# Issue order of expert weight loads, and a second set of raw buffers for the second expert

## The chip, the cores and the metric

One Trainium2 chip, one core. The time of a kernel is the device time of one execution in microseconds (us); the figure for a kernel is the median of its runs. One further execution is recorded by the profiler; its span runs from its first instruction to its last.

## What is computed

Three stages follow each other. Windowed causal attention over 2 x 8 heads of 576 tokens gives 1152 rows of 512 numbers. A dense mixture of four experts follows, and then a routed mixture of eight, in which a row goes to one expert at most:

```
x = attention(q, k, v)                         # window 64, as rows of 512
x = sum over e of p[:, e] * (relu(x @ w1[e]) @ w2[e])          # 4 experts, all rows
keep = x @ w_skip > 0                          # the others leave as they are
e = argmax(x @ w_gate); g = softmax(x @ w_gate)[e]
out[keep] = x + g * (relu(x @ m1[e]) @ m2[e])  # 8 experts, each with its own rows
```

An expert has a first matrix (512 x 1024) and a second one (1024 x 512), 2 MB each in float32.

## The kernel before

Every product is taken with operands split into a high and a low part (`h` and `l`) of float32r, so each weight matrix is loaded raw and then split. A matrix comes in four chunks of 512 KB (`w_load`, one transfer from SP's queue each). `w_split` then has ScalarE (ACT) copy the chunk to the high part (line 331) and VectorE (DVE) subtract to get the low part (line 335). A raw buffer is free again once its low part is written. There are four raw buffers, `raw`; when the routed stage opens (`open_moe2`, key `"M"`), four more, `raw2`, are opened on memory that the dense stage and the routing held.

Two sets of split weights are used in turn: the even routed experts read `wb`, the odd ones `wa`. The weights of expert e + 1 are split while expert e computes (`w_pass("r", e + 1, 1)`, then `(…, 2)`).

An expert works on blocks of 128 of its rows (`block`). TensorE (PE) takes the first product in two pieces of 512 columns, `mm` (line 897); ACT evicts each to `hr` (line 921); PE transposes it (line 938); ACT and DVE write the high and low part of `ht` (lines 942 and 945); PE takes the second product; DVE adds the gated result into `xg` (line 979). Block 0 stands in the straight code of an expert. Blocks 1 and 2 stand behind a branch (`tails`, lines 1086 and 1088) and only run if the expert has that many rows; a last block of at most 64 rows has a shorter form. With these inputs experts 0, 3, 5 and 6 have block 0 alone, experts 1 and 2 have one block more, expert 4 two, and the last expert has one short block.

Rows of an expert are gathered by GpSimd (POOL) from a copy of `x` in device memory (line 847), transposed by PE (line 363), and the results are scattered to the output (line 855).

**The order on the engines is planned.** Each operation is added with an engine, a cost, what it reads and writes, and a priority. `Plan.run` simulates the engines with these costs, and the instructions are issued in the order of their planned start. A load costs 1.46 us on SP, and its reader may start 1.1 us after it. A cast costs (1024 + 112) / 1200 = 0.947 us. On ACT and DVE an operation of priority 0 or more is held back when it would end over 0.2 us after an urgent one (priority below 0, such as the eviction to `hr`) that is already known to be ready. Everything up to the end of expert 0's block 0 is one plan; each later expert's straight part is a plan of its own, which starts at 0.

In these later plans the loads of a first matrix for experts 3 to 7 (`early`) are planned on a made-up engine `"X"`, where each takes 0.01 us; those of the second matrix are planned on `"SP"`. All are issued on SP's queue, which is in order: a load whose buffer isn't free yet holds back every load behind it. The four early loads start at 0.00, 0.01, 0.02 and 0.03, the first load of the second matrix at 0.00. So SP's order is: first matrix, chunk 0; second matrix, chunk 0; first matrix, chunks 1 to 3; second matrix, chunks 1 to 3.

Which buffers a load uses is set by `extra`: for experts 2 to 7 a counter gives the first matrix `raw` and the second `raw2`. Experts 0 and 1 use `raw` for all of their eight chunks.

The routing has its tiles in two pools: `rc`, which stays, and `rt`, which is closed when the routed stage opens. By the tiles' sizes (bytes per partition) the dense stage's pool gives back 43,008, and the routed stage takes 18,432 and 20,480 of it, so 4,096 are left there: one `raw2` buffer lies on the dense stage's memory (`x2`), and three on that of `rt`.

Of the kernel before, what the change touches and what calls it, by code (L numbers as in the profile page):

```python
# [7 lines left out]
F32 = mybir.dt.float32  # L8
F32R = mybir.dt.float32r
BF16 = mybir.dt.bfloat16  # L10
# [13 lines left out]
E2 = 8  # L24
# [175 lines left out]
def c_dve(n):  # L200
    return (n + 64) / 960.0
# [3 lines left out]
def fused_kernel(ctx: ExitStack, tc: tile.TileContext, q, k, v, dp, w1, w2, wskip, wgate, m1, m2, out):  # L205
# [19 lines left out]
    ps_o = attn.enter_context(tc.tile_pool(name="ps_o", bufs=1, space=PSUM))  # L225

    ident = const.tile([128, 128], F32, name="ident")
    identb = const.tile([128, 128], BF16, name="identb")
    mask = [const.tile([128, 128], BF16, name=f"mask{i}") for i in range(2)]
    mask0 = [const.tile([128, 128], BF16, name=f"mask0{i}") for i in range(2)]  # L230
    fold2 = const.tile([128, 64], F32, name="fold2")
    prob = const.tile([128, TT, E1], F32, name="prob")
    psum1 = const.tile([128, TT], F32, name="psum1")
# [10 lines left out]
        "2h": ringa.tile([128, FC, DM], F32R, name="wa2h"),  # L244
        "2l": ringa.tile([128, FC, DM], F32R, name="wa2l"),
    }
    qz = [qk_p.tile([128, HP, 2, 2, 64], F32, name=f"qz{i}") for i in range(2)]
    kt = [qk_p.tile([128, HP, 3, 64], F32, name=f"kt{i}") for i in range(2)]

# [60 lines left out]
    def w_load(src, part, c, prio, extra=False, early=False):  # L310
        b = (M["raw"] if extra else raw_r).buf()

        def f():
            if part == 1:
                SP.dma_start(out=b.tile, in_=src[c * 128:(c + 1) * 128, :])  # L315
            else:
                SP.dma_start(out=b.tile.rearrange("p (a n) -> p a n", a=2),
                             in_=src[c * 256:(c + 1) * 256, :].rearrange("(a p) n -> p a n", p=128))

        add("X" if early else "SP", 0.01 if early else 1.46, f, rd=["M"] if extra else [], new=[b], prio=prio)  # L320
        return b

    def w_split(b, ring, key, part, c, prio, pool=False, after=(), hpool=False, hdve=False):
# [246 lines left out]
    def open_routing():  # L570
        attn.close()
        ps_r = route_ps.enter_context(tc.tile_pool(name="ps_r", bufs=1, space=PSUM))
        rc_p = ctx.enter_context(tc.tile_pool(name="rc", bufs=1))
        rings[0]["1h"] = rc_p.tile([128, KC, FF], F32R, name="wb1h")
        rings[0]["1l"] = rc_p.tile([128, KC, FF], F32R, name="wb1l")
        rt_p = routing.enter_context(tc.tile_pool(name="rt", bufs=1))
        R["rtp"] = rt_p
        R["tab"] = ps_r.tile([128, TT, 5, E2], F32, name="tab")
        R["lg"] = ps_r.tile([128, 512], F32, name="lg")
        R["pf"] = ps_r.tile([128, 512], F32, name="pf")  # L580
        for nm, sh, dt in (("tri", [128, 128], BF16), ("ones", [128, 128], BF16), ("iota_s", [128, 128], F32),
                           ("iota_e", [128, E2], F32), ("jlow", [128, TT + 1], F32), ("tok1", [128, 1], F32),
                           ("wr", [128, KC, E2 + 1], F32), ("os0", [128, E2], BF16), ("os1", [128, E2], BF16),
                           ("cnt", [128, E2 + 2], I32), ("idg", [128, TT, E2], U32), ("ids", [128, TT, E2], U32), ("id0", [128, 1], U32), ("x0", [128, DM], F32),
                           ("gates", [128, TT, E2], F32), ("tb", [128, TT, 5, E2], F32),
                           ("a", [128, TT, E2], F32), ("b", [128, TT, E2], F32), ("lvw", [1, E2], F32),
                           ("lvt", [1, 6, E2], F32), ("lvx", [1, 6, E2], F32), ("lvs", [1, 2], F32)):
            R[nm] = (rt_p if nm in ("tri", "ones", "iota_s", "iota_e", "jlow", "tok1", "wr", "id0", "x0") else rc_p).tile(
                sh, dt, name=nm)
        for i in range(2):  # L590
            for nm, sh, dt in (("x2t", [128, KC, 128], F32), ("m8", [128, 8], F32),
                               ("i8", [128, 16], U32), ("sc", [128, 8], F32), ("oh", [128, E2], BF16),
                               ("ex", [128, E2], F32), ("tm", [128, E2], F32), ("gj", [128, TT + 1], F32),
                               ("oj", [128, TT], F32), ("r", [128, 128], BF16), ("g", [128, 4], F32),
                               ("gb", [128, 4], BF16), ("w", [128, 5, E2], BF16),
                               ("wx", [128, TT, 5 * E2], BF16)):
                R[nm, i] = rt_p.tile(sh, dt, name=f"{nm}{i}", tag=f"{nm}{i}", bufs=1)
        R["rpr"].pool = rt_p

    def route_consts():  # L600
# [24 lines left out]
    def route(t):  # L625
# [108 lines left out]
        def spread(c0, c1, pr, after=()):  # L734

            e0, n = c0 * E2, (c1 - c0) * E2
            add("DVE", c_dve(TT * n) + 0.01, lambda: DVE.tensor_tensor(
                out=T("wx")[:, :, e0:e0 + n],
                in0=T("w")[:, c0:c1].rearrange("p c e -> p (c e)").unsqueeze(1).to_broadcast([128, TT, n]),
                in1=T("oj").unsqueeze(2).to_broadcast([128, TT, n]), op=ALU.mult),  # L740
                rd=[K("oj")] + [K("w0")] * (c0 == 0) + [K("w1")] * (c1 == 5), wr=[K(("wx", c0))], prio=pr)
            add("PE", max(0.11, TT * n / 2400), lambda: PE.matmul(
                out=R["tab"].rearrange("p j c e -> p j (c e)")[:, :, e0:e0 + n], lhsT=T("r"), rhs=T("wx")[:, :, e0:e0 + n],
                start=(t == 0), stop=(t in (GT, TT - 1)), skip_group_check=True),
                rd=[K("r"), K(("wx", c0)), *after], wr=[("tab", c) for c in range(c0, c1)], prio=pr, slack=sl)

# [41 lines left out]
    def route_end():  # L788
        o = R_os(TT - 1)

        def idx():
            tb, a = R["tb"], R["a"]
            DVE.tensor_scalar(out=tb[:, :, 1], in0=R["tab"][:, :, 1], scalar1=128.0, scalar2=-1.0, op0=ALU.mult, op1=ALU.add)
            DVE.tensor_tensor(out=a, in0=tb[:, :, 1], in1=R["tab"][:, :, 0], op=ALU.add)
            DVE.tensor_scalar(out=R["idg"], in0=a, scalar1=0.0, scalar2=None, op0=ALU.max)

        add("DVE", 0.45, idx, rd=[("tab", 0), ("tab", 1)], wr=["idg"], prio=-1)
        for f in later:
            f()
        add("PE", 0.03, lambda: PE.matmul(out=R["pf"][:, 0:E2], lhsT=R["ones"], rhs=R[o], start=True, stop=True),  # L800
            rd=[o], wr=["pf"], prio=-4)

        def num():
            n, x, sm = R["pf"][0:1, 0:E2], R["lvx"], R["lvs"]
            DVE.tensor_tensor(out=x, in0=n.unsqueeze(1).to_broadcast([1, 6, E2]), in1=R["lvt"], op=ALU.is_gt)
            DVE.tensor_reduce(out=sm[:, 1:2], in_=x[:, 5], axis=AX.X, op=ALU.max)
            DVE.scalar_tensor_tensor(out=x, in0=x, scalar=1.0, in1=R["lvw"].unsqueeze(1).to_broadcast([1, 6, E2]),
                                     op0=ALU.mult, op1=ALU.mult, accum_out=sm[:, 0:1])
            DVE.tensor_copy(R["cnt"][0:1, E2:E2 + 2], sm)
            DVE.tensor_copy(R["cnt"][0:1, 0:E2], n)  # L810

        def rest():
            tb, a, b = R["tb"], R["a"], R["b"]
            DVE.tensor_copy(tb[:, :, 2:5], R["tab"][:, :, 2:5])
            DVE.tensor_tensor(out=b, in0=tb[:, :, 2], in1=tb[:, :, 3], op=ALU.add)
            DVE.tensor_tensor(out=R["gates"], in0=b, in1=tb[:, :, 4], op=ALU.add)
            DVE.tensor_scalar(out=b, in0=a, scalar1=0.0, scalar2=4097.0, op0=ALU.is_lt, op1=ALU.mult)
            DVE.tensor_tensor(out=R["ids"], in0=a, in1=b, op=ALU.add)

        add("DVE", 0.84, num, rd=["pf"], wr=["cnt"], prio=16)  # L820
        add("DVE", 1.25, rest, rd=["idg"] + [("tab", c) for c in range(2, 5)], wr=["gates", "ids"], prio=20)


# [163 lines left out]
    def w_pass(kd, e, p, prio=None):  # L987
        if prio is None:
            npass[0] += 1
            prio = 500.0 + 10 * npass[0]  # L990
        src = ((w1, w2) if kd == "m" else (m1, m2))[p - 1][e]
        ring, key = (wa, "wa") if kd == "m" else (rings[e], rkey[e % 2])
        for c in range(4):
            extra = False
            if kd == "r" and e > 1:
                extra = nw[0] % 8 > 3
                nw[0] += 1
            st = KN["w2s"] if (kd, e, p) == ("m", 0, 2) else 2.5
            b = w_load(src, p, c, prio + st * c, extra, early=kd == "r" and e > 2 and p == 1)
            w_split(b, ring, key, p, c, prio + st * c, pool=(kd, e, p) == ("m", 0, 2) and KN["w2pool"][c],  # L1000
                    after=["idg"] if kd == "r" and e == 1 else [])

    nw = [0]

    with tc.manual_schedule():
        w_pass("m", 0, 2, KN["w2p"])
# [158 lines left out]
```

## Time and profile before

| what | value |
|---|---|
| median of 3 runs | 675.88 us (675.45 to 675.97) |
| the profiled execution: time | 672.51 us |
| the profiled execution: span | 670.8 us |
| mean granted clock of TensorE, as a share of full | 0.984 |
| busy share of PE, DVE, ACT, POOL | 94%, 48%, 35%, 14% |

The profiled execution lies 3.37 us below the median, and its span 1.7 us below its time. The busy share of PE is an average: it counts as busy in every slice from about 70 us to 480, where the dense stage ends, and has gaps in the routed stage.

### The profile page before, as it was taken

Reading aid. Unit: us, or ns where it says so; the run is one execution under the profiler, and the core shown is the slowest. Engines: PE = TensorE matmul, PEld = TensorE weight load, DVE = VectorE, ACT = ScalarE, POOL = GpSimd, SP = SyncE. Lnnn points to the kernel's source line nnn. Section 1 sums busy time; section 2 is a strip of 40 time slices with the busy share of each in tenths; the row PEclk is TensorE's granted clock in tenths of the full one; section 3 lists DMA queues with packets and bytes.
Section 4 is the critical chain, followed back from the end, with each engine's and each line's share of the span. In section 5 each row is a group of like instructions: output and inputs, shape, how many; then the busy total and the mean of one; then the engine's idle time right before and its main releaser. Section 6 shows DMA issues by size and latency. Waiting matters only on the chain. (4 is left out here: it accounts for less than half of the span.)

```text
span 670.8 us, 9656 instructions
## 1 busy us (share of the span) xinstructions
PE 628.2 (94%) x3652; PEld 552.8 (82%) x3652; DVE 323.8 (48%) x699; ACT 237.0 (35%) x492; POOL 91.5 (14%) x112
## 2 busy tenths in 40 slices
PE   6889999999999999999999999999987899899783
PEld 6788899898989898989898989898965678687573
DVE  5997932137312136212136336265576575654661
ACT  4974741035202033202033202124326465634550
POOL 6541320000000000000000000000043142312510
PEclk9999999999999999999999999999989999899987
DMA  9668000008300005200004210113339957961631
GB/s 219 159 164 241 23 4 1 0 1 270 106 1 1 0 1 176 75 1 1 0 1 165 87 64 33 48 47 104 129 131 308 360 185 227 303 252 39 209 112 29
DMA packets 55851, 71.69 MB, mean 107 GB/s; under 512 B 32953, under 2 KB 32953, under 8 KB 55776
## 3 DMA queue, kind: packets, MB, share of 16 engines
q1 hardware_dynamic: 52912, 62.17, 29.1%
q0 software_dynamic: 2864, 8.54, 4.4%
q8 instruction: 44, 0.72, 0.4%
q14 instruction: 31, 0.25, 0.1%
HBM read 64.00 MB, written 7.47 MB: 107 GB/s over the span
## 5 line engine op out<-in xcount | busy, mean ns | idle before, releaser
L523 PE MATMUL mm<-xth,wa1h 128*128 128x384 f32 (+1 forms) x416 | 137.4, 330 | 0.0
L523 PE MATMUL mm<-xtl,wa1h 128*128 128x384 f32 (+1 forms) x416 | 135.3, 325 | 0.0
L523 PE MATMUL mm<-xth,wa1l 128*128 128x384 f32 (+1 forms) x416 | 135.2, 325 | 0.0
L529 ACT ACTIVATE hh<-mm 128x384 fp32r<-128x384 f32 (+1 forms) x104 | 48.5, 466 | 234.5 <-PE mm L523 225.9
L544 PE MATMUL mm<-wa2h,hh 128*128 128x512 f32 (+1 forms) x296 | 116.9, 395 | 0.0
L544 PE MATMUL mm<-wa2h,hl 128*128 128x512 f32 (+1 forms) x296 | 115.0, 389 | 0.0
L544 PE MATMUL mm<-wa2l,hh 128*128 128x512 f32 (+1 forms) x296 | 114.9, 388 | 0.0
L531 DVE SCALAR_TENSOR_TENSOR hl<-mm,hh 128x384 fp32r<-128x384 f32 (+1 forms) x104 | 54.5, 526 | 121.7 <-ACT hh L529 121.6
L523 PEld LDWEIGHTS mm<-xth,wa1h 128*128 128x128 f32 x416 | 78.3, 188 | 0.7
L523 PEld LDWEIGHTS mm<-xtl,wa1h 128*128 128x128 f32 x416 | 78.2, 188 | 0.5
L523 PEld LDWEIGHTS mm<-xth,wa1l 128*128 128x128 f32 x416 | 78.2, 188 | 0.0
L544 PEld LDWEIGHTS mm<-wa2h,hl 128*128 128x128 f32 x296 | 55.7, 188 | 12.4
L544 PEld LDWEIGHTS mm<-wa2l,hh 128*128 128x128 f32 x296 | 55.8, 189 | 11.1
L544 PEld LDWEIGHTS mm<-wa2h,hh 128*128 128x128 f32 x296 | 55.8, 188 | 11.0
L556 DVE SCALAR_TENSOR_TENSOR x<-mm,prob,x 128x512 f32<-128x512 f32 (+1 forms) x28 | 20.5, 732 | 91.2 <-PE mm L544 91.2
L766 POOL DMA_INDIRECT x<-scr,id x1 | 1.2, 1242 | 360.3 <-DVE id L783 360.3
L331 ACT CAST wa2h<-raw 128x1024 fp32r<-128x1024 f32 x32 | 33.3, 1053 | 28.0 <-PE mm L544 18.6
L335 DVE TENSOR_TENSOR wa1l<-raw,wa1h 128x1024 fp32r<-128x1024 f32 x31 | 36.9, 1220 | 9.6 <-ACT wa1h L331 9.0
L335 DVE TENSOR_TENSOR wa2l<-raw,wa2h 128x1024 fp32r<-128x1024 f32 x30 | 36.2, 1219 | 7.0 <-ACT wa2h L331 6.8
L331 ACT CAST wa1h<-raw 128x1024 fp32r<-128x1024 f32 x30 | 30.3, 1047 | 22.5 <-DMA raw<-in_moe_w_dram 16.0
L855 POOL DMA_INDIRECT out_dram<-xg,ids x11 | 16.1, 1460 | 86.9 <-DVE xg L979 59.5
L444 POOL TENSOR_TENSOR s<-s,mx 128x512 f32<-128x512 f32 x18 | 20.2, 1122 | 50.1 <-DVE mx L441 23.0
(203 smaller groups left out, 917.8 us busy)
## 6 DMA issues: line engine op xcount, KB each, us to landing
raw<-in_moe_w_dram SPq DMA_DIRECT2D x96, 512.0 KB, 5.5
scr<-x SPq DMA_DIRECT2D x9, 256.0 KB, 2.1
out_dram<-x SPq DMA_DIRECT2D x9, 256.0 KB, 2.3
qn<-in_q_dram SPq DMA_DIRECT2D x8, 256.0 KB, 4.0
kn<-in_k_dram SPq DMA_DIRECT2D x8, 256.0 KB, 4.1
vn<-in_v_dram SPq DMA_DIRECT2D x8, 256.0 KB, 4.7
qn<-in_q_dram SPq DMA_DIRECT2D x2, 128.0 KB, 4.4
kn<-in_k_dram SPq DMA_DIRECT2D x2, 128.0 KB, 4.4
```

The source lines that it names most:

```text
L331: (POOL.tensor_copy if hpool else DVE.tensor_copy if hdve else ACT.copy)(out=aps()[0], in_=b.tile)
L335: (POOL if pool else DVE).tensor_tensor(out=l, in0=b.tile, in1=f32(h), op=ALU.subtract)
L444: add("POOL", 1.0, lambda: POOL.tensor_tensor(out=s.tile, in0=s.tile, in1=mx[:, 3].unsqueeze(2).to_broadcast([128, HP, 128]), op=ALU.mult) ...
L523: PE.matmul(out=ps[:, 0:n], lhsT=wa[a][:, kk, f * 128:(f + 1) * 128], rhs=x[:, kk, g0:g0 + n], start=(i == 0), stop=(i == 3 * KC - 1))
L529: add("ACT", c_act(n), lambda: ACT.activation(out=hh[:, f, 0:n], in_=ps[:, 0:n], func=ACTF.Relu), rd=[ps], wr=[("hh", f)], prio=-1)
L531: add("DVE", c_dve(n), lambda: DVE.scalar_tensor_tensor(out=hl[:, f, 0:n], in0=ps[:, 0:n], scalar=0.0, in1=f32(hh[:, f, 0:n]), op0=ALU.max ...
L544: PE.matmul(out=ps[:, 0:c1 - c0], lhsT=x[:, f, o:o + 128], rhs=wa[a][:, f, c0:c1], start=(f == 0 and i == 0), stop=(f == FC - 1 and i == 2))
L556: DVE.scalar_tensor_tensor(out=z, in0=y, scalar=prob[:, t, e:e + 1], in1=z, op0=ALU.mult, op1=ALU.add)
L766: add("POOL", 1.0, lambda: POOL.indirect_dma_start(out=R["x0"], out_offset=None, in_=scr[0:128 * (GT + 1), :], in_offset=bass.IndirectOffs ...
L855: add("POOL", 1.0, lambda: POOL.indirect_dma_start(out=out, out_offset=bass.IndirectOffsetOnAxis(ap=R["ids"][0:n, j, e:e + 1], axis=0), in ...
```

## The change

The early loads take 0.00 us instead of 0.01 in the plan. The counter is gone: the second matrix of every expert but expert 0 goes into `raw2`, so that expert 1 uses all eight raw buffers as the later ones do. So that `raw2` can be written while the routing is being finished, the routing's tiles that are still in use at that point move from `rt` to `rc` (a new `wy` holds the late part of `wx`); to make room, two masks and an identity move to the pool of the attention, and `tb` is cut from five columns to two, with its sums read from PSUM.

```diff
-    identb = const.tile([128, 128], BF16, name="identb")
-    mask = [const.tile([128, 128], BF16, name=f"mask{i}") for i in range(2)]
-    mask0 = [const.tile([128, 128], BF16, name=f"mask0{i}") for i in range(2)]
+    identb = qk_p.tile([128, 128], BF16, name="identb")
+    mask = [qk_p.tile([128, 128], BF16, name=f"mask{i}") for i in range(2)]
+    mask0 = [qk_p.tile([128, 128], BF16, name=f"mask0{i}") for i in range(2)]
...
-        add("X" if early else "SP", 0.01 if early else 1.46, f, rd=["M"] if extra else [], new=[b], prio=prio)
+        add("X" if early else "SP", 0.0 if early else 1.46, f, rd=["M"] if extra else [], new=[b], prio=prio)
...
-                           ("gates", [128, TT, E2], F32), ("tb", [128, TT, 5, E2], F32),
+                           ("gates", [128, TT, E2], F32), ("tb", [128, TT, 2, E2], F32),
...
-                               ("wx", [128, TT, 5 * E2], BF16)):
-                R[nm, i] = rt_p.tile(sh, dt, name=f"{nm}{i}", tag=f"{nm}{i}", bufs=1)
+                               ("wx", [128, TT, 5 * E2], BF16), ("wy", [128, TT, 3 * E2], BF16)):
+                R[nm, i] = (rt_p if nm in ("x2t", "m8", "i8", "tm", "gj", "wx") else rc_p).tile(sh, dt, name=f"{nm}{i}", tag=f"{nm}{i}", bufs=1)
...
+            wx = lambda: T("wy" if c0 else "wx")[:, :, 0:n]
...
-            tb, a, b = R["tb"], R["a"], R["b"]
-            DVE.tensor_copy(tb[:, :, 2:5], R["tab"][:, :, 2:5])
-            DVE.tensor_tensor(out=b, in0=tb[:, :, 2], in1=tb[:, :, 3], op=ALU.add)
-            DVE.tensor_tensor(out=R["gates"], in0=b, in1=tb[:, :, 4], op=ALU.add)
+            a, b = R["a"], R["b"]
+            DVE.tensor_copy(b, R["tab"][:, :, 2])
+            DVE.tensor_tensor(out=b, in0=b, in1=R["tab"][:, :, 3], op=ALU.add)
+            DVE.tensor_tensor(out=R["gates"], in0=b, in1=R["tab"][:, :, 4], op=ALU.add)
...
-            extra = False
-            if kd == "r" and e > 1:
-                extra = nw[0] % 8 > 3
-                nw[0] += 1
+            extra = kd == "r" and e > 0 and p == 2
```

## Rows read from the trace of the kernel before

**Rows 1.** The page's head: the span.

```profile
span 670.8 us, 9656 instructions
```

**Rows 2.** Waits of PE from 535 us on: total us, times, longest us.

```profile
PE pt L938 <- ACT hr L921: 8.1, 2, 5.4
```

**Rows 3.** Timeline of PE from 560 us: start, us, line, operation, count, idle before.

```profile
560.73 0.51 PE L897 MATMUL mm<-wa1h,xs 128*128 128x512 f32 x1 [0.50 <-PEq L1088]
...
574.20 0.48 PE L897 MATMUL mm<-wb1h,xs 128*128 128x512 f32 x1 [0.23 <-PEq L1086]
...
581.78 1.12 PE L938 MATMUL pt<-ident,hr 128*128 128x128 f32 x4 [2.71 <-ACT hr L921]
...
591.49 0.39 PE L897 MATMUL mmx<-wb1h,xs 128*128 128x512 f32 x1
...
603.52 0.60 PE L363 MATMUL pt<-ident,xj 128*128 128x128 f32 x4
...
615.24 0.39 PE L897 MATMUL mm<-wa1h,xs 128*128 128x512 f32 x1
...
628.53 0.48 PE L897 MATMUL mm<-wb1h,xs 128*128 128x512 f32 x1
...
638.83 1.11 PE L938 MATMUL pt<-ident,hr 128*128 128x128 f32 x4 [5.42 <-ACT hr L921]
...
650.03 0.47 PE L897 MATMUL mm<-wa1h,xs 128*128 128x512 f32 x1 [0.89 <-DVE xg L979]
```

**Rows 4.** Timeline of ACT in expert 6, 628 to 648 us.

```profile
634.54 1.04 ACT L331 CAST wa1h<-raw 128x1024 fp32r<-128x1024 f32 x1 [4.98 <-DMA raw<-in_moe_w_dram]
...
638.19 0.59 ACT L921 ACTIVATE hr<-mm 128x512 f32<-128x512 f32 x1
...
647.08 1.07 ACT L331 CAST wa2h<-raw 128x1024 fp32r<-128x1024 f32 x1
```

**Rows 5.** Timeline of SP's queue, 618 to 632 us: issues, not transfers.

```profile
618.13 0.34 SPq L315 DMA_DIRECT2D raw<-in_moe_w_dram  x1
626.08 0.37 SPq L317 DMA_DIRECT2D raw<-in_moe_w_dram  x1
626.50 1.62 SPq L315 DMA_DIRECT2D raw<-in_moe_w_dram  x3
628.31 3.52 SPq L317 DMA_DIRECT2D raw<-in_moe_w_dram  x3
```

**Rows 6.** Timeline of DVE, 616 to 626 us: the splits of expert 6.

```profile
616.89 4.62 DVE L335 TENSOR_TENSOR wb1l<-raw,wb1h 128x1024 fp32r<-128x1024 f32 x4
...
624.73 1.28 DVE L335 TENSOR_TENSOR wb2l<-raw,wb2h 128x1024 fp32r<-128x1024 f32 x1
```

**Rows 7.** Loads of second matrices issued from 490 to 520 us.

```profile
DMA to landing us min/median/max: 4.6/7.2/12.5
```

**Rows 8.** Timeline of PE from the end of the routing to expert 2.

```profile
485.81 0.61 PE L710 MATMUL mm<-rp,x 128*128 128x128 f32 x4
...
490.86 0.24 PE L742 MATMUL tab<-wx,r 128*128 128x144 bf16 x1
...
507.55 0.47 PE L897 MATMUL mm<-wa1h,xs 128*128 128x512 f32 x1 [2.96 <-PEq L1086]
...
522.29 0.40 PE L897 MATMUL mmx<-wa1h,xs 128*128 128x512 f32 x1
...
536.75 0.51 PE L897 MATMUL mm<-wb1h,xs 128*128 128x512 f32 x1 [0.44 <-PEq L1088]
```

**Rows 9.** Timeline of ACT: a cast in 455:490, an eviction in 490:530.

```profile
467.79 1.05 ACT L331 CAST wa1h<-raw 128x1024 fp32r<-128x1024 f32 x1 [2.91 <-DMA raw<-in_moe_w_dram]
...
490.13 0.60 ACT L921 ACTIVATE hr<-mm 128x512 f32<-128x512 f32 x1 [3.01 <-PE mm L897]
```

**Rows 10.** Timeline of SP's queue: the load of that cast.

```profile
463.32 2.60 SPq L315 DMA_DIRECT2D raw<-in_moe_w_dram  x3
```

**Rows 11.** Branches of line 1086 from 495 to 512 us: count, ns, start.

```profile
L1086 PEldq COMPARE_BRANCH  x1: 6509/6509/6509, 500.9 to 500.9; - x1
```

More of the change, by code (lines that the diff above doesn't have):

```diff
@@ L736, in spread @@
             e0, n = c0 * E2, (c1 - c0) * E2
+            wx = lambda: T("wy" if c0 else "wx")[:, :, 0:n]
             add("DVE", c_dve(TT * n) + 0.01, lambda: DVE.tensor_tensor(
-                out=T("wx")[:, :, e0:e0 + n],
+                out=wx(),
                 in0=T("w")[:, c0:c1].rearrange("p c e -> p (c e)").unsqueeze(1).to_broadcast([128, TT, n]),
@@ L742, in spread @@
             add("PE", max(0.11, TT * n / 2400), lambda: PE.matmul(
-                out=R["tab"].rearrange("p j c e -> p j (c e)")[:, :, e0:e0 + n], lhsT=T("r"), rhs=T("wx")[:, :, e0:e0 + n],
+                out=R["tab"].rearrange("p j c e -> p j (c e)")[:, :, e0:e0 + n], lhsT=T("r"), rhs=wx(),
                 start=(t == 0), stop=(t in (GT, TT - 1)), skip_group_check=True),
@@ L1001, in w_pass @@
                     after=["idg"] if kd == "r" and e == 1 else [])
-    nw = [0]
     with tc.manual_schedule():
```

## Prediction, on record before the changed kernel was seen

> **What bounds the kernel now.** I read the page's head first: a span of 670.8 us in which TensorE counts as busy almost throughout, so only what keeps PE waiting can shorten it [rows 1]. The change touches the routed stage alone, so I took the waits of PE from 535 us on: 8.1 us in two waits of the transposes of line 938 for the eviction `hr` on ACT, the longer of them 5.4 us [rows 2]. The timeline of PE shows where: 2.71 us ahead of 581.78, in expert 4, and 5.42 us ahead of 638.83, in expert 6 [rows 3]. These are the experts that follow one with block 0 alone.
>
> Next, why `hr` is late. In expert 6 ACT evicts `hr` at 638.19, just behind a cast of the next expert's first matrix, and an earlier of those casts had ACT idle for 4.98 us until its load landed [rows 4]. SP's queue says why the load was late: the first chunk of expert 7's first matrix is issued at 618.13, then one of its second matrix at 626.08, and only then, from 626.50, the other three chunks of the first [rows 5]. They had had buffers long before: the low parts that free `raw` are written from 616.89 to 621.51, while the `raw2` buffer on which the queue stood still is freed by the split at 624.73, which lasts 1.28 us [rows 6]. So three loads stood for 5 to 7 us behind a load that they don't need. In expert 4 the order of the queue is the same.
>
> **The early loads at 0.00 us.** The five loads now tie at 0, priority decides, and the first matrix has the smaller numbers: its four chunks come first. No instruction is added or removed; three SP issues move ahead of one, and the one moved back waits for its own buffer until about 626 in any case. POOL's queue isn't touched.
>
> What it is worth is read from whole experts, since a matmul after a wait is slower at first too (four transposes take 1.11 us behind the 5.42 us wait, and 0.60 us at 603.52 [rows 3]). Start to start, experts 3 and 5 take 574.20 - 560.73 = 13.47 and 628.53 - 615.24 = 13.29 us, mean 13.38. Expert 4's block 0 takes 591.49 - 574.20 = 17.29, an excess of 3.91. Expert 6 takes 650.03 - 628.53 = 21.50, of which 0.89 is another wait, for DVE, that stays: an excess of 7.23 [rows 3]. Together **-11.1 us**. From below: if only the waits themselves went, 8.1 [rows 2]. Will the chunks be there? With expert 6's splits ending by 621.5 they would be issued by then, and even the median landing of crowded loads, 7.2 us [rows 7], brings the last at 628.7, when expert 6 begins and ACT takes chunk 0 first.
>
> **`raw2` for expert 1: the gain.** Its second matrix no longer waits for `raw`, and the loads of expert 2's first matrix, which come behind it on SP, find `raw` free earlier. Expert 1's block 0 takes 522.29 - 507.55 = 14.74, 1.36 over the mean; its second block takes 536.75 - 522.29 less the 0.44 of the branch, 14.02 [rows 8], against 603.52 - 591.49 = 12.03 for the same block of expert 4 [rows 3], 1.99 over. With the casts' data there early I take both away: **-3.3 us**. Bounds: none of it, or all.
>
> **`raw2` for expert 1: the price.** This is the part that speaks against the change. The planner believes that the loads land 2.56 us after `"M"` (1.46 + 1.1), so it may put the first cast of `wa2h` at 2.56 to 3.51 us. Block 0's eviction `hr` is planned about 3.38 us after `"M"` (0.264 + 0.2 for the rows' cast, 12 matmuls of 512 columns at 0.215, 0.11 for a table matmul, 0.22 latency). The overrun is 0.13 us, under the 0.2 that the rule allows: the cast goes ahead of `hr` on ACT, and the later casts between the evictions to `ht` and `hr`. All these figures only set the order. What it costs is how late the cast's load lands, for behind it on ACT stand `hr` and `ht` of expert 0, and for those PE's transposes and second product wait.
>
> The load can't go before its buffer is free. The trace doesn't show that wait. From below, the last reader of `x2` ends at 485.81 + 0.61 = 486.4; from above, the last table matmul that reads a tile left in `rt` ends at 490.86 + 0.24 = 491.1 [rows 8]. I take the middle, 488.8, since one buffer lies on `x2` and three on `rt`. Landing takes 467.79 - 463.32 = 4.5 us for a first load after a pause [rows 9, 10], which this one is too; the bound above is 12.5, the largest in the crowd [rows 7]. The cast takes 1.05. So `hr` starts at 488.8 + 4.5 + 1.05 = 494.3 instead of 490.13 [rows 9], and expert 0 ends later by **+4.1 us**; bounds 486.4 + 4.5 + 1.05 = 492.0, +1.8, and 491.1 + 12.5 + 1.05 = 504.7, +14.5. I stay near the lower one because the gathers, which make the crowd, are issued only behind it.
>
> The Trainium skill ("DMA: Bandwidth & Descriptors", section "Anatomy of one DMA") fits a transfer as about 2.0 us plus its bytes / 436e3. For 512 KB that is an estimate of 3.2 us, 1.3 less than the row shows, and the sum below would be -11.6 by it. The fit is for transfers that POOL issues; I keep the row.
>
> **At nothing.** The rest of the diff moves tiles and leaves three small vector instructions on fewer columns where there were three. They lie beside expert 0's second product, long ahead of the gated add that needs them. Without that cover they would still be no more than before.
>
> **The sum:** -11.1 - 3.3 + 4.1 = **-10.3 us**. The profiled execution took 672.51 us, so it would take 662.2. The median of the runs is 3.37 above that execution; I carry this over: 675.88 - 10.3 = **665.5 us**.
>
> **Rivals.**
>
> 1. *The casts stand longer in front of expert 0.* If the buffer comes at the upper bound, 491.1, and the load lands among the gathers at the median of 7.2, `hr` starts at 499.4, 9.2 late: -11.1 - 3.3 + 9.2 = -5.2, **670.7**. For it: three of four buffers lie on the routing's memory. Against: the queues are nearly empty then.
> 2. *The second matrix takes the place of the first.* Its loads are no earlier, and PE is. Expert 7's last is issued by 628.31 + 3.52 = 631.8 [rows 5]; its cast stands at 647.08 [rows 4] and would come at 639.8, which leaves 8.0 us to land. The median is 7.2, the largest 12.5 [rows 7], so up to 4.5 could be given back: **670.0**. Against: with the first matrix out of the way these loads are alone.
> 3. *The wait behind expert 0 goes too.* PE stands 2.96 us ahead of expert 1 [rows 8], and its branch lasted 6.5 us [rows 11] while the loads of expert 1 and the gathers were under way. The loads being done earlier, it could be short: -13.3, **662.6**. The sum leaves it as it is, since expert 2's loads now fall there. The Trainium skill ("Runtime: NRT & Kernel Launch", section "Instruction fetch mechanics") says that a taken branch whose target isn't at hand waits for a DMA to fetch it. By that rule the wait follows the traffic; the one row here fits, but doesn't prove it.
> 4. *Slower.* One mechanism: the first cast of `wa2h` waits on ACT for its load, and all of expert 0 behind it. If it is very late, the low parts that free `raw` are late as well, and expert 1 gains nothing. Then a loss over 11.1 + 1.4 makes the kernel slower by 0.2%: `hr` after 490.13 + 12.5 = 502.6, the load landed after 501.6, 10.5 us behind the latest issue. That is inside the largest landing of 12.5 [rows 7]; at the bound +14.5 - 11.1 = +3.4, **679.3**. Against: the landing would have to be more than twice that of the nearest row.
> 5. *The change doesn't do what it says.* If the tie fell the other way, SP's order would stay and the two parts for expert 1 cancel, +0.8: no change. Priorities speak against it.
>
> **How the numbers follow.** Forecast 0.50; rival 1 0.16; rival 2 0.12; rival 3 0.13; rival 4 0.06; rival 5 0.03. The predicted time is the forecast's, 665.5. The best sum of the bounds is -11.1 - 3.3 + 1.8 - 3.0 = -15.6, 660.3; rivals 1 and 2 end at 670.7 and 670.0. The range from 660.3 to 670.7 holds the forecast, rival 3 and about two thirds of rivals 1 and 2. About 0.2%, 1.35 us, is what a measurement of this kernel tells from no change: faster 0.91, the same 0.03, slower 0.06.
>
> **What the new profile would show.** SP's timeline should have four issues of line 315 together, then four of 317, in every expert from the third on. PE should have no wait over 0.5 us for `hr` in experts 4 and 6, and their block 0 should take about 13.4 us. On ACT a cast of `wa2h` should stand ahead of expert 0's first `hr`, which should start near 494, and PE should reach expert 1 about 4 us later than 507.55. Expert 1's blocks should take about 13.4 and 12.0 us. I am wrong if the casts of `wa2h` stand behind expert 0's evictions (then 4.1 us too slow), if experts 4 or 6 still wait for a load, or if the branch ahead of expert 1 moves by more than 2 us.

## The result and the profile after

The changed kernel takes **664.29 us** (median of 4 runs, 661.88 to 665.74), the kernel before, run beside it, 675.66 (673.43 to 675.97): ratio **0.986 [0.982, 0.990]**. Faster, as forecast; 665.5 had been predicted, and the range held it. The profiled execution took 664.32 us.

The page's head, after, answers to [rows 1]:

```profile
span 662.6 us, 9667 instructions
```

The span is 8.2 us shorter. SP's queue, after (start, us, line; issues, not transfers), answers to [rows 5]:

```profile
492.75 1.92 SPq L317 DMA_DIRECT2D raw<-in_moe_w_dram  x4
505.40 5.50 SPq L315 DMA_DIRECT2D raw<-in_moe_w_dram  x4
...
615.40 3.73 SPq L315 DMA_DIRECT2D raw<-in_moe_w_dram  x4
623.28 5.81 SPq L317 DMA_DIRECT2D raw<-in_moe_w_dram  x4
```

Four issues of line 315 now stand together, then four of 317: no load of a first matrix stands behind one of a second. At 492.75 are the four early loads of expert 1's second matrix. The timeline of PE, after, answers to [rows 3, 8]; lines from 736 on are moved by one:

```profile
488.42 0.51 PE L898 MATMUL mm<-wb1h,xs 128*128 128x512 f32 x1 [0.47 <-ACT xs L875]
...
498.26 1.12 PE L939 MATMUL pt<-ident,hr 128*128 128x128 f32 x4 [4.66 <-ACT hr L922]
...
511.91 0.47 PE L898 MATMUL mm<-wa1h,xs 128*128 128x512 f32 x1
...
525.07 0.40 PE L898 MATMUL mmx<-wa1h,xs 128*128 128x512 f32 x1
...
537.76 0.51 PE L898 MATMUL mm<-wb1h,xs 128*128 128x512 f32 x1 [0.44 <-PEq L1084]
...
561.37 0.50 PE L898 MATMUL mm<-wa1h,xs 128*128 128x512 f32 x1 [0.43 <-PEq L1084]
...
575.70 0.48 PE L898 MATMUL mm<-wb1h,xs 128*128 128x512 f32 x1 [1.09 <-PEq L1082]
...
588.83 0.39 PE L898 MATMUL mmx<-wb1h,xs 128*128 128x512 f32 x1
...
625.79 0.48 PE L898 MATMUL mm<-wb1h,xs 128*128 128x512 f32 x1
...
634.33 0.63 PE L939 MATMUL pt<-ident,hr 128*128 128x128 f32 x4 [0.85 <-DVE ht L946]
...
641.76 0.48 PE L898 MATMUL mm<-wa1h,xs 128*128 128x512 f32 x1 [1.73 <-DVE xg L980]
```

The kernel before started expert 0 here:

```profile
486.90 0.51 PE L897 MATMUL mm<-wb1h,xs 128*128 128x512 f32 x1 [0.47 <-ACT xs L874]
```

So 1.52 us of the span were lost ahead of the routed stage. The tie alone, without the moved tiles, starts expert 0 at 488.71, and other kernels with them at 487.05: this is the scatter of the stage before. Within the routed stage, from 486.90 to 650.03 and from 488.42 to 641.76, the change takes 9.8 us away. The forecast was 10.3. Start to start:

| us | before | after | difference | predicted |
|---|---|---|---|---|
| expert 0 | 20.65 | 23.49 | +2.84 | +4.1 |
| expert 1, block 0 | 14.74 | 13.16 | -1.58 | -1.36 |
| expert 1, second block | 14.46 | 12.69 | -1.77 | -1.99 |
| expert 3 | 13.47 | 14.33 | +0.86 | 0 |
| expert 4, block 0 | 17.29 | 13.13 | -4.16 | -3.91 |
| expert 6 | 21.50 | 15.97 | -5.53 | -7.23 |

ACT at expert 0, after, answers to [rows 9]:

```profile
496.67 1.04 ACT L331 CAST wa2h<-raw 128x1024 fp32r<-128x1024 f32 x1 [8.02 <-DMA raw<-in_moe_w_dram]
497.62 0.59 ACT L922 ACTIVATE hr<-mm 128x512 f32<-128x512 f32 x1
```

The cast of `wa2h` stands ahead of `hr`, and ACT waits 8.02 us for its load. On the scale of before `hr` would have come at 490.13 + 1.52 = 491.65: it is 5.97 late. PE's branches behind expert 0 and ahead of expert 7, after (count, ns, start), then the latter before:

```profile
L1082 PEldq COMPARE_BRANCH  x1: 473/473/473, 508.1 to 508.1; - x1
...
L1056 PEldq COMPARE_BRANCH  x1: 1272/1272/1272, 640.3 to 640.3; - x1
```

```profile
L1060 PEldq COMPARE_BRANCH  x1: 350/350/350, 649.5 to 649.5; - x1
```

The 6.5 us branch of [rows 11] is now 0.47, and the wait of 2.96 ahead of expert 1 is gone. The one ahead of expert 7 went from 0.35 to 1.27. PE's wait of 1.73 at 641.76 is put down to the gated add `xg`, but 640.3 + 1.27 = 641.57 comes 0.19 before the first matmul. In all fourteen profiles of this study that matmul starts 0.1 to 0.2 us behind the end of this branch: the branch ends the wait, whatever the bracket names. What the branch itself waits for is read below.

### The profile page after: what moved, and what is told of

It reads as the page before. It is cut to its first block, busy times and chain, and to the rows that moved or that the text cites. A ratio compares the mean times of both kernels' runs of the same rounds, so it can differ in the third digit from the quotient of the medians.

```text
span 662.6 us, 9667 instructions
## 1 busy us (share of the span) xinstructions
PE 629.0 (95%) x3652; PEld 553.9 (84%) x3652; DVE 322.7 (49%) x699; ACT 236.0 (36%) x492; POOL 93.2 (14%) x112
## 5 line engine op out<-in xcount | busy, mean ns | idle before, releaser
L544 PEld LDWEIGHTS mm<-wa2h,hh 128*128 128x128 f32 x296 | 55.8, 188 | 11.1
L946 DVE SCALAR_TENSOR_TENSOR ht<-pt,ht 128x512 fp32r<-128x512 f32 (+2 forms) x27 | 15.1, 569 | 29.3 <-ACT ht L943 24.4
L856 POOL DMA_INDIRECT out_dram<-xg,ids x11 | 19.0, 1725 | 72.6 <-DVE xg L980 46.9
```

What stands on the lines that cost most here:

```text
L544: PE.matmul(out=ps[:, 0:c1 - c0], lhsT=x[:, f, o:o + 128], rhs=wa[a][:, f, c0:c1], start=(f == 0 and i == 0), stop=(f == FC - 1 and i == 2))
L856: add("POOL", 1.0, lambda: POOL.indirect_dma_start(out=out, out_offset=bass.IndirectOffsetOnAxis(ap=R["ids"][0:n, j, e:e + 1], axis=0), in ...
L946: add("DVE", c_dve(w * n), lambda: DVE.scalar_tensor_tensor(out=ht[:, s, n:2 * n], in0=p[:, 0:w, 0:n], scalar=0.0, in1=f32(ht[:, s, 0:n]), ...
```

## The experiments

Interval ratios are against the kernel before, run on the same chip.

**The parts, one by one.** `e1_no_tie` is the changed kernel with the old cost of the early loads, `e2_tie_only` the kernel before with the new one:

```
-        add("X" if early else "SP", 0.0 if early else 1.46, f, ...
+        add("X" if early else "SP", 0.01 if early else 1.46, f, ...
```

> The changed kernel with the early loads back at 0.01 us in the plan, so only the raw2 part of the change is left. Theory A (the two parts are independent; the tie alone shortens experts 4 and 6, and for expert 1 price and gain about cancel): the waits of PE for hr in experts 4 and 6 come back with 2.7 and 5.4 us, the price at expert 0 (+5.7), the shorter branch (-2.8) and the gain in expert 1 (-3.4) leave -0.5, so 675 us, within 1.5 us of the kernel before. Rival B (raw2 carries most of the gain because everything behind expert 1 then has its loads ahead): 666 to 670 us.

> The kernel before with one number changed, 0.01 to 0.0. Theory A: no wait over 0.5 us for a load in experts 4 and 6, expert 4 shorter by 4.1 and expert 6 by 5.5 to 7.2 us, -9.7 to -11.3 in all: 664.4 to 666 us, as fast as the whole change. Rival B: 671 us or more. Expert 0 and expert 1 are as before: hr of expert 0 without a cast ahead of it, and 1.4 and 2.0 us lost in expert 1's two blocks.

> The changed kernel once more beside the others on this chip. All theories: 664 us. Its profile tells which steps move from one execution to the next: by theory A expert 1 starts 4 us later than before and expert 6 is 5.5 us shorter; whether the branch behind expert 0 is short (0.5 us) and the one behind expert 3 long (4.3 us) again is open.

Measured: without the tie 671.56 us, 0.998 [0.996, 1.001]; the tie alone 665.45, 0.989 [0.986, 0.992]; the changed kernel again 665.23, 0.988 [0.984, 0.991]. The tie carries the whole gain; the eight buffers for expert 1 are worth nothing that can be told. Without the tie SP's queue and PE's waits are those of before:

```profile
616.92 0.34 SPq L315 DMA_DIRECT2D raw<-in_moe_w_dram  x1
624.86 0.37 SPq L317 DMA_DIRECT2D raw<-in_moe_w_dram  x1
625.28 1.63 SPq L315 DMA_DIRECT2D raw<-in_moe_w_dram  x3
```

```profile
PE pt L939 <- ACT hr L922: 7.8, 2, 5.4
```

One issue of line 317, then three of 315 some 8 us behind the first: PE waits 7.8 us for `hr` again, where it waited 8.1 [rows 2].

**Is the price at expert 0 the order of ACT's casts?** `e3_casts_later` gives expert 1's second casts a planner's dependency on expert 0's second product and adds them behind block 0, so they stand behind its evictions. The loads stay early.

```
-        add(... "ACT", ..., hi, rd=[b], wr=[(key, part, "h", c)], prio=prio)
+        add(... "ACT", ..., hi, rd=[b, *hold], wr=[(key, part, "h", c)], prio=prio)
...
+                    hold=[("g2", 0)] if (kd, e, p) == ("r", 1, 2) else [])
```

> The changed kernel with the four casts of expert 1's second matrix held back in the plan until expert 0's second product has begun; the loads stay early. Theory A (what delays expert 0 is the cast that stands ahead of hr on ACT and waits for its load): hr of expert 0 starts 6 us earlier, near 491.6 on the profile's scale, and expert 0 ends 5.6 us earlier. If the branch behind expert 0 stays short that is 658.6 us; if its wait of 3 us comes back, 661.6. Rival C (the routing's vector work would hold expert 0's second product anyway): 664.3 us, no change.

Measured: 665.43 us, 0.989 [0.985, 0.993], the same as the changed kernel. `hr` of expert 0 came on time, 3.23 us behind the start at 488.20 as in the kernel before, and expert 0 still took 24.07 us. ACT's `hr`, PE's waits and its branch:

```profile
491.43 0.60 ACT L922 ACTIVATE hr<-mm 128x512 f32<-128x512 f32 x1 [3.00 <-PE mm L898]
```

```profile
501.61 1.09 PE L363 MATMUL pt<-ident,xg 128*128 128x128 f32 x4 [2.67 <-DMA xg<-scr,idg]
...
512.27 0.48 PE L898 MATMUL mm<-wa1h,xs 128*128 128x512 f32 x1 [2.39 <-PEq L1082]
```

```profile
L1082 PEldq COMPARE_BRANCH  x1: 6054/6054/6054, 506.1 to 506.1; - x1
```

So the order is not all of the price: with it gone a gather and the branch hold PE instead, while the DMA engines are 1.01 busy from 500 to 506.

**Traffic or order?** `e6_small_loads` is the changed kernel, `e7_small_casts_later` the one just shown, both with expert 1's early second loads cut to 32 of 512 columns; casts and low parts read these repeated, so their work keeps its size and expert 1's result is not the right one.

```
+                n = 32 if small else DM
-                SP.dma_start(out=b.tile.rearrange("p (a n) -> p a n", a=2),
-                             in_=src[c * 256:(c + 1) * 256, :].rearrange(...))
+                SP.dma_start(out=b.tile.rearrange("p (a n) -> p a n", a=2)[:, :, 0:n],
+                             in_=src[c * 256:(c + 1) * 256, 0:n].rearrange(...))
```

> The changed kernel, but the four early loads of expert 1's second matrix bring 32 of 512 columns (32 KB each in place of 512), and the casts and low parts read these columns repeated, so that the engines' work keeps its size; the second matrix of expert 1 is not the right one. It takes away their traffic and leaves the order of the casts. Theory A (order of the casts): what keeps expert 0's `hr` is the buffer, free at 492.75 on SP, and the cast behind it; only the landing shrinks, from 3.9 to about 2.3 us. So `hr` starts about 1.6 us earlier than 497.62, near 496, and expert 0 takes about 22 us, still more than the 20.7 of before. Rival B (traffic): without the 2 MB the gathers and the code behind expert 0 come at once, and expert 0 takes at most 20.7 us, as before, although its casts stand where they did.

> The kernel with expert 1's second casts held behind expert 0, and in addition its four early loads at 32 of 512 columns, with the casts and low parts reading these repeated; the second matrix of expert 1 is not the right one. With the full loads expert 0 took 24.07 us although `hr` came on time: 2.67 us of wait for a gather and 2.39 for the branch. Theory A (the traffic of 2 MB keeps gather and branch): both waits go, to under 0.5 us each, and expert 0 takes 24.07 - 2.67 - 2.39 = about 19 us, less than the 20.7 of before. Rival B (the gathers and the branch are late by themselves, since they are issued or reached late): expert 0 stays within 1 us of 24.07.

Measured: 662.15 us, 0.986 [0.983, 0.989], and 657.92, 0.979 [0.977, 0.981]. Expert 0 and 1 by order and traffic, start to start, with PE's own work in expert 0 (from its start to the idle time ahead of expert 1), over all profiles:

| us | expert 0 | PE's work in it | experts 0 and 1 |
|---|---|---|---|
| buffers as before (four profiles) | 17.70 to 20.77 | 16.7 to 17.8 | 49.7 to 50.2 |
| casts ahead of `hr`, 512 KB loads (seven) | 22.34 to 23.59 | 20.9 to 23.4 | 48.8 to 49.5 |
| casts behind `hr`, 512 KB loads | 24.07 | 21.7 | 51.5 |
| casts ahead of `hr`, 32 KB loads | 18.96 | 18.5 | 45.6 |
| casts behind `hr`, 32 KB loads | 18.92 | 17.8 | 44.8 |

The traffic costs 3.4 to 5.2 us in expert 0, the order alone, start to start, nothing that adds up. What expert 0 loses by the eight buffers, expert 1 gains: together they take 0.2 to 1.4 us less with them.

With the small loads and the casts in front, ACT and PE show:

```profile
494.60 1.04 ACT L339 CAST wa2h<-raw 128x1024 fp32r<-128x1024 f32 x1 [6.05 <-DMA raw<-in_moe_w_dram]
495.55 0.59 ACT L931 ACTIVATE hr<-mm 128x512 f32<-128x512 f32 x1
```

```profile
496.19 0.66 PE L948 MATMUL pt<-ident,hr 128*128 128x128 f32 x4 [2.69 <-ACT hr L931]
```

`hr` is still 4.0 us late (495.55 against 488.32 + 3.23, expert 0's start here and `hr`'s distance from it in the kernel before), as theory A said, but PE waits 2.69 instead of 4.66, and expert 0 ends where rival B put it. The windows of the changed kernel, then of the small loads (PE, PEld, DVE, ACT and POOL busy, granted clock, DMA share, GB/s), show the rest:

```profile
488.00:496.00 8.00, 5.18 (x22) 3.71 (x22) 4.18 (x27) 0.64 (x2) 1.47 (x2) 1.00 0.28 64
496.00:504.00 8.00, 5.05 (x17) 3.86 (x18) 2.67 (x12) 5.68 (x8) 5.32 (x6) 0.58 1.02 380
504.00:512.00 8.00, 7.85 (x32) 6.12 (x31) 7.86 (x13) 1.73 (x3) 0.00 (x0) 0.78 0.75 235
```

```profile
488.00:496.00 8.00, 5.19 (x22) 3.72 (x22) 4.18 (x27) 1.95 (x4) 1.56 (x2) 1.00 0.12 21
496.00:504.00 8.00, 6.60 (x35) 4.96 (x36) 6.09 (x20) 5.17 (x8) 6.47 (x6) 1.00 0.67 196
```

In the 8 us in which the wait of 4.66 us ends the granted clock is 0.58, much of it at the lower of the two levels; where the wait of 2.69 ends it stays at 1.00. PE has 17 entries there against 35. Part of the price is therefore a slower PE; that the longer wait alone makes it so is not shown, since the clock is 0.79 in these 8 us in the kernel before and in `e7_small_casts_later` too, with no wait over 1.4 us. These kernels bring 2 MB less in all, so 18.9 us bounds what moving the traffic could give; no run here moves it. My condition that both waits go was met for the gather; of the branch 1.1 us was left. It lasted 4.0 and 4.6 us in these two, with the 2 MB gone: the early loads are not its only cause.

**What is left in expert 6: VectorE's order?** There VectorE writes two low parts of its own second matrix, then four of the next first matrix, ahead of `ht`; the timeline of DVE, after:

```profile
626.35 2.35 DVE L335 TENSOR_TENSOR wb2l<-raw,wb2h 128x1024 fp32r<-128x1024 f32 x2
628.96 4.63 DVE L335 TENSOR_TENSOR wa1l<-raw,wa1h 128x1024 fp32r<-128x1024 f32 x4 [0.26 <-PE mm L898]
633.51 0.68 DVE L946 SCALAR_TENSOR_TENSOR ht<-pt,ht 128x512 fp32r<-128x512 f32 x1
```

`e4_dve_known` tells the planner of that backlog, `e5_tie_dve` does so in the kernel with the tie alone:

```
-OFF = dict(DVE=1.0, ACT=0.1)
+OFF = dict(DVE=3.2, ACT=0.1)
```

> The changed kernel, but the planner is told that VectorE is busy for 3.2 us at the start of each routed expert from the first on, in place of 1.0. By its own plan the low part `ht` then goes ahead of the third and fourth low part of the next first matrix. Theory A: the waits of PE for `ht` (0.85 us) and the longer wait for the gated add `xg` (1.73 in place of 0.89) in expert 6 come from that order alone. Then expert 6 takes 15.97 - 0.85 - 0.84 = about 14.3 us, experts 2, 3 and 5 stay within 0.3 us, and the kernel is 1 to 2 us shorter than the changed one. Rival B: VectorE is behind with its sum of work, not its order. Then each expert leaves one more low part to the next, the wait only moves to the gated add, expert 6 stays within 0.5 us of 15.97 and the kernel within 0.7 us of the changed one.

> The kernel before with the five early loads at 0.00 us, and VectorE's first 3.2 us told to the planner in place of 1.0; nothing else of the change. The tie alone took experts 0 and 1 to 50.2 us together and expert 6 to 16.2. Theory A (VectorE's order): expert 6 falls to about 14.5 us and the kernel comes 1 to 2 us below the tie alone, to 0.986 to 0.987 of the kernel before, the best so far. Rival B (VectorE's sum of work): within 0.7 us of the tie alone, 0.989.

Measured: 667.51 us, 0.992 [0.989, 0.995], and 665.6, 0.991 [0.988, 0.994]: no gain. The wait for `ht` is gone as planned, and PE's own work in expert 6 falls from 14.2 to 13.2 us in both. But PE then stands 4.30 us ahead of expert 7, and 2.3 instead of 1.1 behind expert 3. Two branches lie ahead of expert 7 (lines as in the changed kernel): line 1082's, for further blocks of expert 6, and line 1056's, for a whole or a short block of expert 7. PE and both, with VectorE's backlog known:

```profile
642.85 0.55 PE L898 MATMUL mm<-wa1h,xs 128*128 128x512 f32 x1 [4.30 <-DVE wa2l L335]
```

```profile
L1082 PEldq COMPARE_BRANCH  x1: 4018/4018/4018, 635.3 to 635.3; - x1
...
L1056 PEldq COMPARE_BRANCH  x1: 3077/3077/3077, 639.6 to 639.6; - x1
```

The branches again, 4.02 and 3.08 us one behind the other, and not the low part that the bracket names. They took back what the order gave; neither theory had them.

**VectorE's sum of work?** `e8_pool_one`, `e9_pool_two` and `e10_tie_pool_one` put the last one or two low parts of each second matrix on GpSimd; `e11_low_short` writes the last one for 8 of 1024 columns on VectorE.

```
-            ... pool=(kd, e, p) == ("m", 0, 2) and KN["w2pool"][c],
+            ... pool=(kd, e, p) == ("m", 0, 2) and KN["w2pool"][c] or kd == "r" and e > 1 and p == 2 and c == 3,
```

The second has `c >= 2` there; the third is the first's line in the kernel with the tie alone. The fourth:

```
             h, l = aps()
+            if short:
+                DVE.tensor_tensor(out=l[:, 0:8], in0=b.tile[:, 0:8], in1=f32(h)[:, 0:8], op=ALU.subtract)
+                return
...
+                    short=kd == "r" and e > 1 and p == 2 and c == 3)
```

> The changed kernel, with the low part of the last chunk of each second matrix from expert 2 on made by GpSimd in place of VectorE. Another order on VectorE did not help expert 6, so the theory now is that its sum of work keeps PE there: 14.18 us busy in the 16 us from 626 to 642. Theory A (sum of work): one low part less, about 1.15 us, shortens the waits for `ht` (0.85) and for the gated add (0.84 over that of before) by that much together; expert 6 falls from 15.97 to about 14.8 us and the kernel is about 1 us shorter, more if expert 3's successor gains too. Rival B (GpSimd's queue): a low part takes 2.35 us there, and behind it stand the gathers of the next rows. Then a wait for `xg` or `pt` on a gather comes in its place, and the kernel is no shorter, or longer.

> The same with the last two chunks on GpSimd. Theory A: two low parts less, 2.3 us, more than both waits together (1.7), so expert 6 ends at about 14.3 us, 0.5 less than with one. Rival B: two low parts take 4.7 us on GpSimd in one go, and the gathers behind them or the second product that needs these low parts come later: PE waits for `wa2l` or `wb2l`, and the kernel is slower than with one.

> The kernel before with the early loads at 0.00 us and the low part of the last chunk of each second matrix from expert 2 on made by GpSimd; expert 1's second matrix as before. If the part with all eight buffers is worth nothing in sum, this lies within 0.3% of the changed kernel with the same low part on GpSimd. Theory A gives about 1 us less than the tie alone (0.989), so 0.987; rival B 0.989 or more.

> The changed kernel, but the low part of the last chunk of each second matrix from expert 2 on is made for 8 of 1024 columns only, still on VectorE and at its place in the order: the output lacks the rest of these corrections, and VectorE has about 1.1 us less to do in each expert, with nothing put on GpSimd. The kernel that moved this work to GpSimd had VectorE's four low parts of the next first matrix take 6.84 us in place of 4.63 while GpSimd made its own. Theory A (VectorE's sum of work keeps PE in expert 6; GpSimd's low part failed because it held VectorE up): the wait for `ht` (0.85) goes and that for the gated add falls to about 0.9, so expert 6 takes 14.3 to 14.9 us in place of 15.97 to 16.4, and the kernel is 1 to 2 us shorter than the changed one. Rival B (the work on VectorE is not what ends last there): expert 6 stays at 15.9 or more.

Measured: 665.73 us, 0.988 [0.986, 0.990]; 666.58, 0.989 [0.987, 0.991]; 666.24, 0.988 [0.986, 0.990]; and 661.97, 0.984 [0.980, 0.988]. No version with GpSimd gains. DVE and POOL, with one low part on GpSimd:

```profile
626.08 6.84 DVE L335 TENSOR_TENSOR wa1l<-raw,wa1h 128x1024 fp32r<-128x1024 f32 x4 [0.26 <-ACT wa1h L331]
```

```profile
628.15 2.55 POOL L335 TENSOR_TENSOR wb2l<-raw,wb2h 128x1024 fp32r<-128x1024 f32 x1
```

VectorE's four low parts take 6.84 us in place of 4.63, 2.21 more, while GpSimd writes one in 2.55. What VectorE gives away it pays back in standing, and PE waits 1.9 us for `ht` where it had waited 0.85. PE's own work in expert 6, from its start to the idle time ahead of expert 7, and the two branches:

| | PE's work in expert 6, us | branch of line 1082, then of line 1056, us |
|---|---|---|
| before; without the tie | 20.6; 20.7 | 0.59, 0.35; 0.43, 0.43 |
| after; again | 14.2; 13.9 | 1.88, 1.27; 2.86, 2.08 |
| tie alone | 14.2 | 1.90, 1.51 |
| backlog known, after; tie alone | 13.2; 13.2 | 4.02, 3.08; 3.32, 2.77 |
| one on GpSimd, after; tie alone | 15.3; 15.3 | 2.72, 1.95; 2.85, 2.31 |
| two on GpSimd | 16.5 | 1.84, 1.15 |
| one low part short | 13.2 | 3.60, 3.25 |

Less work on VectorE does shorten PE's own by 0.7 to 1.1 us, with no wait for `ht` left, as the order alone does; in the profiled run of `e11_low_short` the branches then took 3.60 and 3.25 and gave it back. Its profile is its slowest run, 667.62 us; the others lie from 660.97 to 662.95. Its ratio overlaps that of the changed kernel, so its worth is not settled. None of these kernels beats the changed one by more than the intervals. The two with one low part on GpSimd differ by 0.1%: the eight buffers are worth nothing here either.

**What do the branches wait for?** The traces keep the transfers that bring code, on a queue of their own. From 638.50 to 640.30 in the changed kernel, between the two branches ahead of expert 7, one of them is all that the DMA engines move:

```profile
DMA packets 1, 0.02 MB, mean 9 GB/s; under 512 B 0, under 2 KB 0, under 8 KB 0
...
q8 instruction: 1, 0.02, 3.9%
```

Such a packet has 16 KB and takes 0.9 to 1.6 us. The kernel gives PE a prefetch hint (`hint`) ahead of the branch of line 1082, and none ahead of that of line 1056. By the times of the hints, packets and branches in the traces (us; where there is no hint, the end of the branch before):

| branch | hint | code under way | branch |
|---|---|---|---|
| behind expert 0, before | 498.78 | 504.77 to 505.97 | 500.87 to 507.38 |
| behind expert 0, after | 504.36 | 505.52 to 506.97 | 508.06 to 508.53 |
| line 1082 ahead of expert 7, before | 642.55 | 643.79 to 645.05 | 645.81 to 646.40 |
| line 1056 ahead of expert 7, before | (646.40) | 647.13 to 648.14 | 649.51 to 649.86 |
| line 1082 ahead of expert 7, after | 634.64 | 635.91 to 637.07 | 636.53 to 638.41 |
| line 1056 ahead of expert 7, after | (638.41) | 639.15 to 640.25 | 640.33 to 641.60 |
| line 1082, backlog known | 633.03 | 636.82 to 637.93 | 635.28 to 639.30 |
| line 1056, backlog known | (639.30) | 640.05 to 641.32 | 639.60 to 642.68 |

In the routed stage of the fourteen profiles 77 of these branches last over 1 us, and each ends 1.3 to 1.5 us behind the landing of its packet: PE waits for its code. How long it waits depends on when the packet comes and on when PE gets there. Ahead of expert 7 the packet of line 1056 starts 0.7 to 0.8 us behind the end of line 1082's branch (1.3 in `e11_low_short`), and that branch ends 3.1 to 3.6 us behind the other in all fourteen profiles; its 0.35 to 3.25 us are what is left of this when PE has done its work. Behind a hint the packet starts 1.0 to 6.2 us later. In the 38 cases of 70 in which it came over 2.3 us later the DMA engines were 0.53 to 1.04 busy, from 1 us behind the hint until it started. The loads that the tie moves ahead fall into such stretches: behind expert 5 the packet comes 1.21 us after its hint in both profiles without the tie and 1.6 to 3.9 in the twelve with it, and behind expert 3 3.4 and 3.5 against 3.8 to 6.1, which is most of the 0.86 that expert 3 lost. Behind expert 5 the windows from hint to packet, before and after, show the DMA share (the last but one figure):

```profile
622.60:623.80 1.20, 1.20 (x10) 1.09 (x9) 0.27 (x1) 1.20 (x3) 0.00 (x0) 1.00 0.32 72
```

```profile
619.90:623.10 3.20, 3.20 (x20) 2.75 (x19) 2.30 (x3) 3.20 (x6) 0.00 (x0) 1.00 0.97 356
```

No run gives line 1056 a hint, or another place to one, so what that would bring is open. That the loads are what holds the code back rests on these pairs and on the DMA shares; no run takes the loads away at these places.

## Why the prediction was right

**The early loads at 0.00 us** (-11.1 foretold). Right in mechanism, and the whole gain: SP's order, the loads' times, and no wait for `hr` in experts 4 and 6. Block 0 of expert 4 fell to 13.13, 0.25 below the mean it was measured by. Expert 6 lost 5.53 of 7.23. The step that was mis-sized is that an expert without these waits would take the mean of experts 3 and 5: with `hr` there in time, VectorE's low parts ended last ahead of `ht` (0.85), and the branch ahead of expert 7 took 0.92 more. 5.53 + 0.85 + 0.92 = 7.30. I had put the 0.89 there down to VectorE, as the bracket did, and kept it; it was the branch's, and it grew to 1.73. In the kernel before the code of that branch came while PE was still at work behind its long wait, and only 0.35 us of the branch was left to see. Expert 3's branch gave back 0.86. Together this part measured about 9 us in the profile.

**Expert 1's gain** (-3.3): -1.58 - 1.77 = -3.35, as foretold.

**Expert 0's price** (+4.1): `hr` came 5.97 late where 4.17 was foretold. The buffer came at the upper bound, SP's 492.75 - 1.52 = 491.2, 2.4 later than the middle that I took; the landing took 496.67 - 492.75 = 3.9 in place of 4.5. The cast stands where I said, but the path that I gave for the price, that it costs what the cast's load lands late, is not the main one: with the casts taken away from `hr` the price stays, and with the small loads all but 0.8 us of it goes from PE's own work, although `hr` is 4.0 late. The 2 MB themselves are the larger part, through gather, branch and granted clock; I had taken the gathers alone for the crowd. PE's own work in expert 0 grew by 5.7 us (17.7 to 23.3). That expert 0 grew by 2.84 only is rival 3, which the sum had left out: its branch went, and with it the 2.96. This branch was one of my signs of being wrong, if it moved by more than 2 us; it moved by 6.

The Trainium skill ("Runtime: NRT & Kernel Launch", section "Instruction fetch mechanics") says that a taken branch whose target is not at hand waits for a DMA to fetch it. I had read the traffic into that. The traces bear out both: behind expert 0 the code came 5.99 us behind its hint before, with the DMA engines 1.05 busy in the last 4.9 us of it, and 1.16 us behind it after, where PE passed the hint 5.6 us later. It is not steady: in the seven profiles with this expert 0 the branch took 0.47 to 1.64 us in six and 5.26 in one (`e8_pool_one`), and in the four with the buffers as before 3.20 to 6.51.

**The sum.** In the routed stage -9.8 against -10.3: the price was 1.3 too high, the gain in expert 6 1.7 too high, expert 3's 0.86 unforeseen, the small terms the rest. That it came so near is in part luck: the price on PE's own work was 1.5 too low, and a wait of 2.8 that the sum had kept went. By the medians of two jobs the gain is 11.4 and 7.1 us; the ratios' intervals, 0.982 to 0.991, hold the forecast, 0.985. Rival 1 met its condition (the buffer at the upper bound) without its landing; rivals 2, 4 and 5 did not come.

## What to carry to other kernels

A queue that issues in order lets a load that waits for its buffer hold up every load behind it; read the order of issues beside the times at which buffers come free, and a tie in a planner's costs can be worth more than a doubled ring. Loads that are brought forward take their traffic with them: ask what gather or branch shares those microseconds, not only what stands behind the cast. When a wait goes, the next one in line sets the gain, so a block is better measured against the next engine's work than against a block that follows other neighbours. Where a branch stands between two blocks, look for the transfer of its code, not only for the engine that a wait is named after: here work taken off PE's path was lost again to two branches whose code came late.

## What the runs showed of the hardware

- A branch of PE's queue at one place of the program took 0.35 to 3.25 us in fourteen profiles, and another 0.47 to 6.5; the wait behind it can be named after an engine that had finished before. All 77 that last over 1 us end 1.3 to 1.5 us behind the landing of a 16 KB packet of code, which started 1.0 to 6.2 us behind a prefetch hint, and 0.7 to 1.3 behind the branch before where there was none.
- In the 8 us in which a wait of 4.66 us ended the granted clock was 0.58; where one of 2.69 ended in the same place it stayed at 1.00. It was 0.79 there before, with no wait over 1.4 us, so the wait is not all of it.
- A subtraction of two SBUF operands on GpSimd (2.55 us) lengthened VectorE's four of the same kind by 2.21 us. The Trainium skill ("Trainium Architecture — The Big Picture", section "What this means for kernel authors") calls the port pair that the two share "an exclusive lock (not a bandwidth split)"; these rows agree.
